# Dealing the last zero fill to the transfer engines in four arcs instead of two pieces

## The chip, the cores and the metric

One core of a Trainium2 chip. A core has five engines with queues of their own (TensorE or PE, VectorE or DVE, ScalarE or ACT, GpSimd or POOL, SyncE or SP) and 16 transfer engines that carry all DMAs, numbered 0 to 15 here. A DMA is issued by one of the queues, cut into packets, and the packets are dealt to the transfer engines. The metric is device microseconds of one execution, from the outside; the profile's span, from the first to the last instruction, is a little shorter. An engine "carries" a row when the packets of this row are in its queue.

## The reference

One decode step of a transformer block with adaptive layer norm, forward and backward: the outputs are the block's result and the gradients of it in all ten inputs, in bfloat16.

```python
mod = silu(c) @ w_mod                        # six rows of 1024
h = layernorm(x) * (1 + ca) + sa
q = h @ wq                                   # 32 heads of 128
k, v = the last 4096 of 65536 positions of k_cache, v_cache (4 heads, each used by 8 of q)
x = x + ga * (softmax(q k^T * 128**-0.5) v) @ wo
h = layernorm(x) * (1 + cb) + sb
x = x + gb * ((sigmoid(h @ w_gate) * (h @ w_up)) @ w_down)
out, vjp = jax.vjp(block, ...);  return (out, *vjp(grad_out))
```

Only the last 4096 positions of the caches are read, so the gradients of the caches (out_2 and out_3 of the kernel, 4 heads x 65536 x 128 each) are zero at the first 61440 positions of each head. These zeros are 126 MB of the 185.6 MB that the kernel writes to memory.

## The kernel before, in words

All of it is one long program for one core, in an order written out by hand (`tc.manual_schedule()`): no planner and no loop over tiles decides when something runs. Weights and caches are loaded into one big on-chip tile (`arena`), the forward and backward products run on TensorE, gradients of the weights are outer products that VectorE and ScalarE write into buffers in `arena`, and DMAs store the buffers. Nearly all of these DMAs are issued from GpSimd's queue, some from SyncE's.

Between them come the zeros. They are cut into 120 regions of 1 MB, kept in the list `zleft`; `zero(n)` (line 186) takes the next n regions and issues their fill on GpSimd's queue. Calls of `zero` are strewn over the whole program with counts from tables (`Z_N`, `Z_B`, `Z_ROWS` and others), so that fills are issued where the queues have room. A fill is a DMA from a region already zero to the next (first from an on-chip tile of zeros, later, when `from_dram[0]` is set, from the first region filled, `zero_src`).

Seven of the 120 regions are "narrow": they are 128 rows of 8 KB, with 120 KB from row to row. Their indices in the list are in `NARROW`. Of a narrow region, rows 8 to 127 are filled by the fill proper; rows 0 to 7 of all seven are filled by `zero_rest` (line 424) and by small head DMAs. A narrow fill is there to give the transfer engines unequal work:

- line 193 resets the cursor that says on which transfer engine the next DMA from GpSimd begins;
- line 196 issues the head, a DMA of 256-byte pieces with an outer size of 5 (`NS`), or of 7 (`NL`) in the last narrow fill. An outer size of n takes n engines in a row, and the cursor goes on by n;
- the first six narrow fills then issue 120 rows with an outer size of 60 (line 209). This goes to 15 engines, 8 rows each, beginning at engine 5, and so leaves out engine 4 (`SKIP`);
- the last one (`n == nlen - 1`, lines 200 to 207) issues two pieces. Each is a view `(t p) x -> p t x` with `t = 3`, so its outer size is the rows divided by 3. The first has 72 rows, outer size 24, and goes to 12 engines from engine 7 on (7 to 15 and 0 to 2), 6 rows each. The second has 48 rows, outer size 16, and goes to all 16, 3 rows each. Engines 3 to 6 (`LIGHT`) therefore carry 3 rows, the other twelve 9.

This last narrow fill is the last entry of `zleft`. It is issued by `zero(Z_ROWS[1])` (line 1339), after the store of a piece of the gradient of w_up (`dw_rows`, line 1142) and ahead of the stores of the gradient of wo (`dwo`, line 1274). After it 56 more DMAs go out, 43 of GpSimd (`dw_rows`, `dwo`, `sec` at line 1269, `dwq_tile` at 1315, `s2` at 1319, `kv_store` at 1311) and, near the end, 13 of SyncE. These have an outer size of 128 and load all 16 engines alike, but for three tiny ones with 8 rows (line 308). The last are stores of the key gradient, two from GpSimd's queue and two from SyncE's.

Of the kernel before, what the change touches and what calls it, by code (L numbers as in the profile page):

```python
# [11 lines left out]
FP32 = mybir.dt.float32  # L12
# [22 lines left out]
SCALE = DH ** -0.5  # L35
KIB = 512
SKIP = 4
LIGHT = (3, 4, 5, 6)
NARROW = (15, 45, 75, 93, 103, 113, 119)

# [21 lines left out]
def kernel(  # L63
# [91 lines left out]
    def as_rows(piece, n):  # L155
        return piece.rearrange("i (p x) -> (i p) x", p=n)
# [9 lines left out]
    nlen = len(NARROW)  # L166
    ncount = list(range(1, nlen + 1))
    NS = SKIP + 1
    NL = LIGHT[-1] + 1
    rest = out_2[0, 0, 0:SKW, :].rearrange("r d -> (r d)").rearrange("(p x) -> p x", p=P)[0:8, 0:nlen * ZW].bitcast(FP32)  # L170
    assert nlen * 2 <= 20

# [2 lines left out]
    zero_rows = zero_src[:, 0:P * ZW // 4].rearrange("i (p x) -> (i p) x", p=P).bitcast(FP8)  # L175

    def pairs(rows):
        return rows.rearrange("(t p) x -> p t x", t=2)

    def dep(later, earlier):  # L180
        tc.add_manual_dep(later.ins, earlier.ins.name,
                          mybir.DependencyInfo(mybir.DependencyClass.Sync, mybir.DependencyReason.DATA),
                          reason="pace")

    def zero(n, after=None, big=False):
        for _ in range(n):
            if len(zleft) <= keep[0]:
                return
            region, narrow_ = zleft.pop(0)  # L190
            first = None
            if narrow_:
                nc.gpsimd.inc_swdge_sem([], [], mode="reset_dge_cursor")
                n = nlen - ncount.pop()
                ns = NL if n == nlen - 1 else NS
                first = nc.gpsimd.dma_start(
                    out=rest[0:ns, 0:nlen * 128].rearrange("p (t x) -> p t x", t=2)[:, :, n * 64:(n + 1) * 64],
                    in_=(zero_rows[0:ns, 0:128].rearrange("p (t x) -> p t x", t=2) if from_dram[0] else
                         zeros[0:ns, 0:64].rearrange("p (t x) -> p t x", t=1).broadcast_to([ns, 2, 64])))
                if n == nlen - 1:  # L200
                    a0 = 8
                    for rows in (6 * (16 - len(LIGHT)), 3 * 16):
                        ins = nc.gpsimd.dma_start(
                            out=region[a0:a0 + rows, :].bitcast(FP32).rearrange("(t p) x -> p t x", t=3),
                            in_=zero_rows[0:rows, :].rearrange("(t p) x -> p t x", t=3))
                        a0 += rows
                    assert a0 == P and from_dram[0]
                else:
                    ins = nc.gpsimd.dma_start(
                        out=pairs(region[8:P, :].bitcast(FP32)),  # L210
                        in_=(pairs(zero_rows[0:120, :]) if from_dram[0] else
                             zeros[0:60, :].rearrange("p (t x) -> p t x", t=1).broadcast_to([60, 2, ZW // 2])))
            elif big and region.shape[0] == 1:
                ins = nc.gpsimd.dma_start(  # L214
                    out=as_rows(region, BIGP).bitcast(FP32),
                    in_=zero_src[:, 0:P * ZW // 4].rearrange("i (p x) -> (i p) x", p=BIGP).bitcast(FP8))
            else:
                if region.shape[0] == 1:
                    region = as_rows(region, P)
                if from_dram[0]:  # L220
                    ins = nc.gpsimd.dma_start(out=pairs(region.bitcast(FP32)), in_=pairs(zero_rows))  # L221
                else:
                    ins = nc.gpsimd.dma_start(out=region.bitcast(FP32), in_=zeros[:, :])
            if after is not None:
                dep(first or ins, after)
# [198 lines left out]
    def zero_rest(after):  # L424
# [3 lines left out]
        dep(ins, after)  # L428
        for n0, n1, ns in ((0, nlen - 1, NS), (nlen - 1, nlen, NL)):
            nc.gpsimd.dma_start(  # L430
# [120 lines left out]
    for j in range(KD):  # L551
        if j in (1, 2, 3):
            kT_unit(8 + 2 * j)
            kT_unit(9 + 2 * j)
        if 0 < j <= NT:
            for g in range(G):
                wqT_unit(j - 1, g, "AVAA"[g])
        for b in range(2):
            mm = rows_mm(q_ps[b], h1_bf[:, j:j + 1], heads(wq_t[j])[:, 16 * b:16 * b + 16, :], j == 0, j == KD - 1)
        zero(Z_Q[j], mm)  # L560
# [14 lines left out]
    for ch in range(8):  # L575
        ps = new_ps("sc_ps")
        for g in range(G):
            mm = nc.tensor.matmul(ps[32 * g:32 * g + 32, 0:512], lhsT=q_col2[:, HG * g:HG * g + 32],
                                  rhs=k_T[:, g, ch * 512:(ch + 1) * 512], start=True, stop=True,
                                  tile_position=(0, 32 * g))  # L580
        nc.scalar.copy(out=P_bf[:, ch * 512:(ch + 1) * 512], in_=ps[:, :])
        nc.vector.reduce_max(out=mx8[:, ch:ch + 1], in_=ps[:, :], axis=AX.X)
        zero(Z_KC[ch], mm)
# [25 lines left out]
    rsum = vt([P, 1], "rsum")  # L609
    last = nc.vector.reciprocal(out=rsum, in_=ssum)  # L610
    zero(Z_SM, last)
    from_dram[0] = True
    rs_ps = new_ps("rs_ps")[:, 0:P]
# [709 lines left out]
    for b in range(2):  # L1323
        do4 = new_ps("do4")
        for i in range(KD):
            for a in range(4):
# [4 lines left out]
                       in_=do4.rearrange("q (a h r) -> q a h r", a=4, h=4))  # L1331
# [189 lines left out]
```

## Time and profile before

| | before |
|---|---|
| time, median of 3 runs | 592.18 us (592.12 to 592.22) |
| the profiled execution's own time | 592.17 us |
| its span | 590.4 us |
| PE, DVE, ACT, POOL busy | 73%, 60%, 42%, 26% |
| moved | 246.04 MB in 32030 packets, mean 417 GB/s |
| memory read, written | 88.50 MB, 185.60 MB |
| last narrow fill issued | 459.2 us (head), 460.0 and 460.8 us (the two pieces) |
| its pieces, issue to landing | 10.7 and 10.8 us |
| last compute | about 569 us |

The page gives DMA's busy share as the mean over the 16 transfer engines, so one engine that is busy while the others are done shows as a sixteenth. The queues q0 and q1 are the DMAs of GpSimd and of SyncE; q8 and q14 load instructions. In the table by stretches each row has the stretch, its length, the busy time of PE, weight loads, DVE, ACT and POOL with the number of instructions, then TensorE's granted clock, DMA's share and GB/s. DMA's share can be a little over 1, where packets of two queues overlap.

### The profile page before, as it was taken

The page shows a single profiled execution, that of the slowest core. Times are in us where ns is not written, and L with a number is a line of the kernel's source. Part 1 is how long each engine was busy: PE and PEld are TensorE (multiplying, and loading weights), DVE is VectorE, ACT ScalarE, POOL GpSimd, SP SyncE. Part 2 cuts the span into 40 slices and gives each one's busy share as a digit, 9 for nine tenths or more (in the row PEclk, how much of TensorE's full clock was granted, in tenths as well). Part 3 has the DMA queues.
Part 4 walks back from the last instruction along what each step waited for, and adds up shares of the span by engine and source line. Part 5 has one row for each costly group of instructions (what it writes and reads, how often), then busy time and mean ns, then how long its engine had stood idle before and what let it go on. Part 6 is the DMA issues. An engine that isn't in the chain of part 4 may idle for free.

```text
span 590.4 us, 10143 instructions
## 1 busy us (share of the span) xinstructions
PE 429.2 (73%) x4160; PEld 244.6 (41%) x4160; DVE 354.2 (60%) x646; ACT 248.3 (42%) x398; POOL 152.2 (26%) x253
## 2 busy tenths in 40 slices
PE   3998689999999999997977756665684437175410
PEld 2884333323334545543544645554572336013100
DVE  3765579988931103019471866888886967655750
ACT  2579510545541103411223655666572446074410
POOL 3113214122122212222222322333312733132100
PEclk9997689999999999999998768878757756655555
DMA  8999999999999999999999999999999999999998
GB/s 350 422 419 421 422 455 427 423 428 431 427 399 465 402 443 440 399 441 435 416 391 405 418 412 408 402 411 397 420 420 425 423 426 424 422 418 415 414 412 340
DMA packets 32030, 246.04 MB, mean 417 GB/s; under 512 B 4898, under 2 KB 4904, under 8 KB 16680
## 3 DMA queue, kind: packets, MB, share of 16 engines
q0 software_dynamic: 26992, 225.98, 95.1%
q1 hardware_dynamic: 4944, 19.41, 9.3%
q8 instruction: 32, 0.52, 0.3%
q14 instruction: 14, 0.11, 0.0%
q10 hardware_dynamic: 48, 0.01, 0.0%
HBM read 88.50 MB, written 185.60 MB: 464 GB/s over the span
## 4 chain that ended last, share of the span: by engine, by line
PE 40%; DMA 26%; DVE 17%; ACT 9%; issue 4%; POOL 1%; ACTq 0%; POOLq 0%; DVEq 0%; SPq 0%
PE b_ps L808 15%; DMA out_dram<-arena 12%; PE n_ps L749 9%; DMA arena<-in_B_w_gate_dram 5%; DVE arena L263 4%; DVE arena L250 4%; PE t_ps L703 4%; DMA arena<-in_w_mod_dram 3%; ACT arena L1306 3%; DVE arena L267 3%; DMA arena<-in_B_w_down_dram 2%; DMA out_dram<-out_dram 2%; ACT arena L541 2%; DVE scr L267 2%; PE tp_k L520 1%
## 5 line engine op out<-in xcount | busy, mean ns | idle before, releaser
L808 PE MATMUL b_ps<-arena 128*128 128x512 bf16 x512 | 117.5, 382 | 1.1 <-ACT arena L952 1.1
L250 DVE TENSOR_TENSOR arena<-arena 128x2048 bf16<-128x2048 bf16 (+1 forms) x67 | 78.2, 1177 | 9.0 <-PE n_ps L749 5.2
L952 ACT COPY arena<-tp_side 128x1024 bf16<-128x1024 bf16 x62 | 61.0, 1016 | 52.2 <-PE tp_side L951 51.4
L808 PEld LDWEIGHTS <-arena 128*128 128x128 bf16 x512 | 48.7, 99 | 57.6 <-issue 4.6
L749 PE MATMUL n_ps<-arena 128*128 128x512 bf16 x256 | 67.6, 389 | 3.0 <-DVE arena L250 2.5
L214 POOL DMA_DIRECT2D out_dram<-out_dram x72 | 35.7, 497 | 128.7 <-PE n_ps L749 60.9
L951 PE MATMUL tp_side<-ident_bf,arena 128*128 128x128 bf16 x496 | 49.9, 267 | 9.5 <-DVE arena L250 5.8
L263 DVE TENSOR_SCALAR arena<-arena,slab 128x3584 bf16<-128x3584 bf16 (+2 forms) x40 | 43.5, 1124 | 21.5 <-DMA out_dram<-arena 21.5
L951 PEld LDWEIGHTS <-arena 128*128 128x128 bf16 x496 | 41.8, 123 | 18.3 <-issue 8.5
L711 ACT CAST arena<-t_ps 128x512 bf16<-128x512 f32 x56 | 29.0, 599 | 39.9 <-PE t_ps L703 39.9
L1302 PE MATMUL ps_kv<-arena 32*128 32x512 bf16 x64 | 26.6, 582 | 25.8 <-DVE arena L271 10.0
L267 DVE CUSTOM_DVE_ANT_0 arena<-arena,scr 128x1024 bf16<-128x1024 bf16 x35 | 40.8, 1224 | 0.2
L1306 ACT ACTIVATE arena<-ps_kv 128x512 bf16<-128x512 f32 x48 | 25.0, 716 | 36.0 <-PE ps_kv L1302 18.7
L749 PEld LDWEIGHTS <-arena 128*128 128x128 bf16 x256 | 21.5, 99 | 35.5 <-issue 19.0
L267 DVE CUSTOM_DVE_ANT_0 scr<-arena,b1k 128x1024 bf16<-128x1024 bf16 x28 | 34.2, 1223 | 3.2 <-DMA arena<-in_B_w_down_dram 2.8
L259 DVE CAST arena<-b_ps 128x512 bf16<-128x512 f32 x6 | 4.2, 692 | 48.8 <-PE b_ps L808 48.8
L221 POOL DMA_DIRECT2D out_dram<-out_dram x31 | 18.9, 612 | 30.1 <-DVE rows_all L250 24.4
L703 PE MATMUL t_ps<-arena 128*32 128x512 bf16 x256 | 24.1, 399 | 2.8 <-ACT arena L772 2.8
L1302 PEld LDWEIGHTS <-arena 32*128 32x128 bf16 x64 | 6.8, 112 | 44.4 <-issue 43.6
L541 ACT COPY arena<-tp_wq 128x1024 bf16<-128x1024 bf16 x23 | 21.5, 1071 | 7.3 <-PE tp_wq L539 7.3
L1089 ACT COPY arena<-tp_ug 128x1024 bf16<-128x1024 bf16 x21 | 20.5, 1009 | 6.7 <-PE tp_ug L1088 6.7
L977 POOL DMA_DIRECT2D arena<-in_B_w_up_dram x14 | 10.8, 773 | 42.3 <-DVE slab L267 21.6
(268 smaller groups left out, 659.3 us busy)
## 6 DMA issues: line engine op xcount, KB each, us to landing
out_dram<-arena POOLq DMA_DIRECT2D x35, 1024.0 KB, 14.1
out_dram<-out_dram POOLq DMA_DIRECT2D x31, 1024.0 KB, 13.1
out_dram<-arena POOLq DMA_DIRECT2D x16, 896.0 KB, 17.3
out_dram<-zeros POOLq DMA_DIRECT2D x10, 1024.0 KB, 10.7
arena<-in_A_wq_dram POOLq DMA_DIRECT2D x8, 1024.0 KB, 20.9
arena<-in_A_wo_dram POOLq DMA_DIRECT2D x8, 1024.0 KB, 12.4
arena<-in_w_mod_dram POOLq DMA_DIRECT2D x7, 1024.0 KB, 18.7
arena<-in_B_w_up_dram POOLq DMA_DIRECT2D x14, 512.0 KB, 10.2
```

What stands on the lines that cost most here:

```text
L214: ins = nc.gpsimd.dma_start(out=as_rows(region, BIGP).bitcast(FP32), in_=zero_src[:, 0:P * ZW // 4].rearrange("i (p x) -> (i p) x", p=BIGP ...
L250: return nc.vector.tensor_tensor(out=out, in0=a, in1=b, op=op)
L263: return nc.vector.tensor_scalar(out=out, in0=a, scalar1=s1, scalar2=None, op0=op0)
L267: return nc.vector.tensor_tensor_reduce(out=out, in0=w, in1=b, scale=1.0, scalar=0.0, op0=ALU.mult, op1=ALU.add, accum_out=acc)
L541: nc.scalar.copy(out=blk, in_=tp[:, :])
L703: nc.tensor.matmul(ps[32 * hh:32 * hh + 32, :].rearrange("p (j m) -> p j m", j=4), lhsT=N_sb[:, h * P + a:(h + 1) * P - 3 + a:4], rhs=a4[: ...
L749: mm = nc.tensor.matmul(nbank[k][:, :], lhsT=k_nat[:, g, t_ * DH:(t_ + 1) * DH], rhs=vp[:, t_ % 2, 4 * k:4 * k + 4, :].rearrange("p h d -> ...
L808: mm = nc.tensor.matmul(bbank[p][k][:, :], lhsT=a4[:, p, h, :], rhs=wo_t[u][:, a, k * 512:(k + 1) * 512], start=(i == 0 and a == 0), stop= ...
L951: nc.tensor.transpose(tp[:, i * P:(i + 1) * P], blk[:, i * P:(i + 1) * P], ident_bf[:, :])
L952: nc.scalar.copy(out=blk if dst is None else dst, in_=tp[:, :])
L1302: nc.tensor.matmul(ps[:, :], lhsT=rows[r, t8 * P:(t8 + 1) * P], rhs=bd[r, :], start=True, stop=True, tile_position=(32 * tc_, 0))
L1306: nc.scalar.activation(out=o, in_=v, func=ACT.Copy, scale=float(scale))
```

## The change

The last narrow fill is issued as four DMAs instead of two. `ARCS` lists, in the order of the cursor, how many engines a piece is for and how many rows each of them gets. The view is the same, with `t` equal to the rows of an engine, so that the outer size of a piece is its number of engines. The head still has an outer size of 7, so the first piece begins at engine 7.

| piece | engines | rows each | rows |
|---|---|---|---|
| (2, 11) | 7, 8 | 11 | 22 |
| (6, 7) | 9 to 14 | 7 | 42 |
| (4, 11) | 15, 0, 1, 2 | 11 | 44 |
| (4, 3) | 3 to 6 | 3 | 12 |

The 120 rows, their source and their place in GpSimd's queue are the same.

```diff
-LIGHT = (3, 4, 5, 6)
+FIRST = 7
+ARCS = ((2, 11), (6, 7), (4, 11), (4, 3))
...
-    NL = LIGHT[-1] + 1
+    NL = FIRST
...
                 if n == nlen - 1:
                     a0 = 8
-                    for rows in (6 * (16 - len(LIGHT)), 3 * 16):
+                    for engines, each in ARCS:
+                        rows = engines * each
                         ins = nc.gpsimd.dma_start(
-                            out=region[a0:a0 + rows, :].bitcast(FP32).rearrange("(t p) x -> p t x", t=3),
-                            in_=zero_rows[0:rows, :].rearrange("(t p) x -> p t x", t=3))
+                            out=region[a0:a0 + rows, :].bitcast(FP32).rearrange("(t p) x -> p t x", t=each),
+                            in_=zero_rows[0:rows, :].rearrange("(t p) x -> p t x", t=each))
                         a0 += rows
```

## The prediction

> **What bounds the kernel now.** I read the page first: the time slices, then the queues. The digits are DMA's busy share of each fortieth of the span, and below them what it moved.
>
> ```profile
> DMA  8999999999999999999999999999999999999998
> GB/s 350 422 419 421 422 455 427 423 428 431 427 399 465 402 443 440 399 441 435 416 391 405 418 412 408 402 411 397 420 420 425 423 426 424 422 418 415 414 412 340
> ...
> q0 software_dynamic: 26992, 225.98, 95.1%
> q1 hardware_dynamic: 4944, 19.41, 9.3%
> q8 instruction: 32, 0.52, 0.3%
> ```
>
> The transfer engines are busy from the first slice to the last; no compute engine is over 73%. So this kernel ends when the last of 16 transfer engines has emptied its queue, and what counts is how evenly the work lies on them. The table by stretches shows how it ends (the last two columns are DMA's share and GB/s):
>
> ```profile
> 475.00:500.00 25.00, 14.72 (x240) 13.65 (x244) 17.74 (x31) 14.45 (x21) 8.15 (x11) 0.57 1.01 424
> ...
> 565.00:570.00 5.00, 0.60 (x2) 0.00 (x0) 3.94 (x7) 0.60 (x1) 0.51 (x1) 0.50 1.01 419
> 570.00:580.00 10.00, 0.00 (x0) 0.00 (x0) 0.00 (x0) 0.00 (x0) 0.54 (x2) 0.50 1.01 411
> 580.00:585.00 5.00, 0.00 (x0) 0.00 (x0) 0.00 (x0) 0.00 (x0) 0.00 (x0) 0.50 1.03 423
> 585.00:588.00 3.00, 0.00 (x0) 0.00 (x0) 0.00 (x0) 0.00 (x0) 0.00 (x0) 0.50 0.84 350
> 588.00:590.40 2.40, 0.00 (x0) 0.00 (x0) 0.00 (x0) 0.00 (x0) 0.00 (x0) 0.50 0.03 14
> ```
>
> Compute is over by 570 us; from there on stores drain at full rate until 585, at 0.84 until 588, and then nearly nothing moves. The trace's packet records give the end more finely. They do not name the engine, but while an engine is loaded its next packet starts 3 or 4 ns before the last one ends, so packets can be linked into 16 chains. From about 473 us to 585 us there are always 16 packets under way. The chains end at 585.20, 585.32, then thirteen of them from 587.51 to 588.34, and one alone at 589.11. That last chain sets the end: 1.28 us later the span of 590.39 closes. One engine is thus 0.77 us behind the second last, and two are 3 us ahead of the rest.
>
> Where the fill is issued, GpSimd's timeline (start, length, count, idle before it) and the fill's own line:
>
> ```profile
> 459.20 0.78 POOL L196 DMA_DIRECT2D out_dram<-out_dram  x1
> 459.98 1.59 POOL L203 DMA_DIRECT2D out_dram<-out_dram  x2
> 461.56 4.35 POOL L1274 DMA_DIRECT2D out_dram<-arena  x3
> 467.23 0.53 POOL L1274 DMA_DIRECT2D out_dram<-arena  x1 [1.32 <-DMA out_dram<-arena]
> 469.35 1.03 POOL L1274 DMA_DIRECT2D out_dram<-arena  x1 [1.59 <-DVE arena L263]
> ```
>
> ```profile
> L203 POOL DMA_DIRECT2D out_dram<-out_dram x2: 783/796/809, 460.0 to 460.8; - x2
> ...
> DMA to landing us min/median/max: 10.7/10.7/10.8
> ```
>
> ```profile
> L1274 POOL DMA_DIRECT2D out_dram<-arena x8: 533/652/3288, 461.6 to 489.0; - x8
> ...
> DMA to landing us min/median/max: 11.6/14.3/18.6
> ```
>
> The reader sees that the two pieces take 0.80 us of GpSimd each, and that this and the stores behind it land 10.7 to 18.6 us after issue: about that much work stands in the queues.
>
> **The change, part by part.** Rows per engine, before: 6 of the 72-row piece on engines 7 to 15 and 0 to 2, and 3 of the 48-row piece on all, so 9, and 3 on engines 3 to 6. After: 11 on six of them (7, 8, 15, 0, 1, 2), 7 on 9 to 14, 3 on 3 to 6. The sum is 120 both times (12x9 + 4x3; 6x11 + 6x7 + 4x3), so no byte is added: two rows move from each of six engines to each of six others.
>
> *A row's price.* 419 GB/s in the stretch 565 to 570 is 26.2 GB/s for each of 16 engines, so a row of 8 KB takes 8192/26.2 = 0.313 us; the links of a chain give 0.306 (packets of 8192 bytes start 306 ns apart). I take 0.31; two rows are 0.62 us. From 473 us on the engines are never without a packet, so these 0.62 us go unchanged through the 115 us that follow to that engine's end.
>
> *The end.* It depends on which group the last chain (589.11) is in.
> - In 3 to 6: it stays at 589.11. The worst that a lifted engine can do is 588.34 + 0.62 = 588.96, still before it. Change 0.
> - In 7, 8, 15, 0 to 2: 589.73, change +0.62.
> - In 9 to 14: it falls to 588.49; the next is a lifted one at up to 588.96, so the change is between -0.15 and -0.62.
>
> Followed back to the fill, the last chain looks like one of the four that carry no row of the 72-row piece, which is engines 3 to 6. Two chains can cross within a nanosecond and be swapped, and some are, so this is a lean and no proof; it is why I take 0. Of the two early chains nothing is gained: they wait for the last whatever they carry.
>
> *Two more issues on GpSimd.* 2 x 0.80 = 1.6 us of its time at 460 us, ahead of the eight stores of L1274, the stores of L1142 that are queued between them, and what follows on its queue; SP's queue holds nothing at that time. Hidden: those stores wait 11.6 us or more in the queues before they land, so being issued 1.6 us later only makes that wait shorter. The trace also shows GpSimd's transfers using eight completion semaphores in turn, so a transfer waits for the eighth before it. The reset's head and its pieces now take five of the eight places for 1 MB instead of three. The third store of L1274 then waits for a store issued at 458.59 instead of 449.84, and may go out some 5 us later than its 465.4 (an estimate: the landing of 11.6 us added to 458.59 gives 470.2). Behind that transfer are then the fill and two stores of 1 MB, about 7 us at 423 GB/s, less up to 4 us by which some chains are ahead of others there. Cover remains, though less. Lower bound 0. If it is gone, the engines stand idle for up to the added 1.6 us: upper bound +1.6. I take 0, since 16 packets are under way throughout and the landing rows are far above the delay. Who waits for these stores is VectorE, which reuses their buffers; it idles 21.5 us for DMA in the last 130 us already and has the order of the queue, not the issue time, to thank for it.
>
> *More completions.* Each transfer ends with 16 packets of 4 bytes; two more transfers add 32, which start about 6 ns apart: 0.01 us if spread, 0.2 us if all fall on one engine. I take 0.01, because the before's own completions are spread over the chains.
>
> *Sum:* 0 + 0 + 0.01 on the profiled execution's 592.17 us (span 590.39 and 1.78 around it), which is 0.01 below the median of 592.18. Forecast 592.2.
>
> [...]
>
> **The rivals.**
> *A late engine is loaded further (slower side, within the bound).* The last chain is 7, 8, 15 or 0 to 2, for instance because an engine that the deal holds for light is slow by itself. Price 0.62: 592.8. For it: six of 16 engines are in that group. Against: the chain looks like one without the six rows.
> *The late engine is relieved.* It is one of 9 to 14: 591.55 to 592.0, middle 591.8. For it: again six of 16. Against: the same.
> *The queue runs dry (slower).* Place: 468 to 473 us, where five of the eight places hold 1 MB. It decides when what stands in the queue of the engines furthest ahead falls under the delay of the stores. Price up to 1.6: 593.8. For it: GpSimd already waits for DMA there (1.32 us before the fourth store), and one store takes 3.288 us to issue. Against: 7 us of work less 4 us of lead.
> *The deal isn't what it says.* The four pieces would have to start each where the one before ended. If all began at engine 7, engines 7 and 8 would carry 11 + 7 + 11 + 3 = 32 rows instead of 9: 23 x 0.31 = 7.1 us late, less the 0.77 of a chain that isn't the last: 598.5. Against: before, the 72-row piece starts behind the seven engines of the small head in the records, four chains without it; the cursor is thus kept between transfers.
> *The odd packets fall elsewhere.* 32 instruction loads of 16 KB take about 1 us each of one engine, and the last chain has one of them at 487.3 us. With other code they may fall on other engines: the end then moves between 588.34 and 589.9 by itself, 591.4 to 593.0.
>
> **How the numbers follow.** Unchanged end (592.2): 0.46. Loaded further (592.8): 0.21. Relieved (591.8): 0.13. Odd packets (591.4 to 593.0): 0.08. Queue dry (593.8): 0.07. Wrong deal (598.5): 0.02. What is left, 0.03, I give to a faster end by more than I can find a reason for. 0.2% is 1.18 us, about what a measurement of this kernel tells from no change: 591.0 to 593.36. The first four cases lie inside: 0.88. Slower 0.09, faster 0.03. Range 591.5 to 593.1: it holds the unchanged, loaded and relieved cases and most of the odd packets, and leaves out the dry queue and the wrong deal.
>
> **What would show it.** Right: L203 (under its new line) four times, GpSimd 0.8 us each; 16 packets under way all through; the drain after 570 us the same, the last chain within 0.7 us of 589.1. Wrong: a DMA share under 1.00 in the stretch 460 to 500; or one engine's packets going on for several us after the others have ended; or the early chains gone and the late ones with them.

## The result: 1.7 us slower, outside the predicted range

| | before | after |
|---|---|---|
| median, 16 runs each, taken together | 591.96 us (591.55 to 592.28) | 593.64 us (592.93 to 596.96) |
| ratio | | 1.0039, 95% interval 1.0026 to 1.0051 |
| profiled execution | 592.17 us, span 590.4 | 593.8 us, span 591.7 |
| time outside the span | 1.78 us | 2.12 us (median) |
| last of 16 chains of packets ends | 589.11 us | 590.28 us |

Thirteen of the 16 times of the changed kernel lie between 592.93 and 594.88 us, three between 596.71 and 596.96. The profiled execution is one of the many.

The page of the changed kernel, slices and queues:

```profile
DMA  8999999999999999999999999999999999999997
GB/s 347 421 418 420 421 451 426 431 431 430 426 395 463 407 445 425 405 438 434 431 382 410 417 412 407 395 410 405 421 421 425 420 426 417 417 417 412 413 413 328
DMA packets 32430, 246.04 MB, mean 416 GB/s; under 512 B 5298, under 2 KB 5304, under 8 KB 17080
...
q0 software_dynamic: 27392, 225.99, 95.0%
```

The bytes are the same and the transfer engines are still the bound. But there are 400 more packets (32030 before), all on GpSimd's queue and all under 512 B. I had counted 32. The rest is filling: a piece that goes to n < 16 engines puts on each of the others as many packets of 4 bytes as one of its own engines gets rows. Before, that was 6 x 4 = 24 for the first piece and none for the second; now 11 x 14 + 7 x 10 + 11 x 12 + 3 x 12 = 392. The difference of 368 and the 32 completions make 400. Two other deals below have the counts that this gives, 32398 and 32062 packets (same_rows_four and two_more_even). So has the kernel before: of its 4182 packets of 4 bytes on GpSimd's queue 245 x 16 = 3920 are completions, and 262 are the filling of its seven heads (6 x 22 + 18), of the six narrow fills with 8 rows on each of 15 engines (48), of the first piece (24) and of two small DMAs of `zero_rest` (26 + 14). What the counts show is on how many engines a piece goes and how many rows each gets. The engines' numbers are those of the kernel's own count from the reset, and no record names an engine. That each piece begins where the one before ended is not in the counts either; but had all begun at engine 7, two engines would have ended some 7 us late by my estimate, and the 16 chains end within 3.5 us.

The fill's line and GpSimd's timeline in the changed kernel (first: durations min/median/max; then start, length, count, idle before):

```profile
L205 POOL DMA_DIRECT2D out_dram<-out_dram x4: 767/805/905, 460.6 to 463.1; - x4
```

```profile
460.58 3.27 POOL L205 DMA_DIRECT2D out_dram<-out_dram  x4
465.38 0.71 POOL L1276 DMA_DIRECT2D out_dram<-arena  x1 [1.53 <-DVE arena L265]
467.82 0.56 POOL L1276 DMA_DIRECT2D out_dram<-arena  x1 [1.73 <-DMA out_dram<-arena]
469.93 2.65 POOL L1276 DMA_DIRECT2D out_dram<-arena  x3 [1.54 <-DVE arena L265]
```

Four issues of 0.8 us, as forecast. The stores of dwo (L1274 before, now L1276) go out later: the first three at 461.56, 464.84 and 465.38 before, at 465.38, 467.82 and 469.93 now. The third is 4.5 us late.

The end of the changed kernel, by stretches:

```profile
475.00:500.00 25.00, 14.72 (x236) 13.63 (x237) 17.71 (x31) 14.27 (x21) 8.44 (x11) 0.56 1.01 422
...
580.00:585.00 5.00, 0.00 (x0) 0.00 (x0) 0.00 (x0) 0.00 (x0) 0.00 (x0) 0.50 1.03 421
585.00:588.00 3.00, 0.00 (x0) 0.00 (x0) 0.00 (x0) 0.00 (x0) 0.00 (x0) 0.50 0.90 377
588.00:591.70 3.70, 0.00 (x0) 0.00 (x0) 0.00 (x0) 0.00 (x0) 0.00 (x0) 0.50 0.22 89
```

No engine runs dry for a time that counts (the share stays at 1.01 and above until 585; by the packet records 16 packets are under way at every moment from 460 to 473 us, and fewer in 0.2% of the time from 473 to 585, 0.1% in the kernel before), and yet more is left at the end: 0.22 of 3.7 us after 588, where before it was 0.03 of 2.4. (The share goes over 1 on one queue too: from 475 to 500 us GpSimd's packets alone make 1.009 in the kernel before, and within a chain a packet starts 3 or 4 ns before the last one ends, on one queue as on two.) The packets linked into chains say more. The 16 chains now end in two groups of eight, at 586.76 to 588.44 and at 589.40 to 590.28; their mean is 588.62 instead of 587.73. So 0.9 us of the 1.17 us by which the last end moved is work that all engines do later, and 0.27 is a wider spread.

Where the 0.9 us arose, I read from the packet records: the bytes not yet moved at a given time, as time at 419 GB/s, after minus before. It is 0.12 at 5 us already (other kernels' profiled executions have up to 0.1 us there, and up to 0.5 us at 460 us, ahead of the fill, so only what is added from then on counts), 0.15 at 464, 0.31 at 472, 0.36 at 496, 0.68 at 512 and 0.87 at 560 to 584. So a sixth of a microsecond comes with the fill and a third between 496 and 512, where nothing of the change runs any more. In that stretch packets of 8 KB took 319 ns on the mean instead of 311, as this row of after and this of before show (417 against 424 GB/s at the same share):

```profile
500.00:510.00 10.00, 3.27 (x38) 1.36 (x38) 6.15 (x8) 3.02 (x7) 2.78 (x5) 0.85 1.02 417
```

```profile
500.00:510.00 10.00, 3.20 (x37) 1.26 (x37) 5.94 (x8) 2.84 (x6) 3.54 (x5) 0.84 1.01 424
```

### The profile page after: what moved, and what is told of

Read it like the earlier page. It is cut to its first block, busy times and chain, and to the rows that moved or that the text cites. A ratio compares the mean times of both kernels' runs of the same rounds, so it can differ in the third digit from the quotient of the medians.

```text
span 591.7 us, 10145 instructions
## 1 busy us (share of the span) xinstructions
PE 429.4 (73%) x4160; PEld 243.2 (41%) x4160; DVE 354.1 (60%) x646; ACT 247.8 (42%) x398; POOL 150.7 (25%) x255
## 2 busy tenths in 40 slices
DMA packets 32430, 246.04 MB, mean 416 GB/s; under 512 B 5298, under 2 KB 5304, under 8 KB 17080
## 4 chain that ended last, share of the span: by engine, by line
PE 42%; DMA 23%; DVE 16%; ACT 9%; issue 5%; POOL 1%; ACTq 0%; POOLq 0%; DVEq 0%
PE b_ps L810 15%; DMA out_dram<-arena 14%; PE n_ps L751 9%; DMA arena<-in_B_w_gate_dram 5%; DVE arena L252 4%; PE t_ps L705 4%; DVE scr L269 3%; DMA arena<-in_w_mod_dram 3%; DVE arena L265 3%; ACT arena L1308 3%; ACT arena L543 2%; DVE arena L269 2%; PE tp_side L953 2%; PE fg L1067 1%; PE tp_k L522 1%
## 5 line engine op out<-in xcount | busy, mean ns | idle before, releaser
L1304 PE MATMUL ps_kv<-arena 32*128 32x512 bf16 x64 | 26.6, 581 | 26.4 <-DVE arena L265 10.2
```

Source lines behind the costliest of these rows:

```text
L1304: nc.tensor.matmul(ps[:, :], lhsT=rows[r, t8 * P:(t8 + 1) * P], rhs=bd[r, :], start=True, stop=True, tile_position=(32 * tc_, 0))
```

## The experiments

Times are medians; each is compared with runs of the kernel before taken beside it (592.02 to 592.23 us). "Outside" is time less span.

| kernel | pieces of the last fill | time, us | ratio, 95% interval | outside, us |
|---|---|---|---|---|
| same_rows_four | 4 | 598.73 | 1.0069 to 1.0133 | 2.12 |
| two_more_even | 4 | 597.12 | 1.0073 to 1.0099 | 2.15 |
| new_rows_base | 4 | 594.73 | 1.0039 to 1.0064 | 2.12 |
| mirrored | 4 | 600.24 | 1.0076 to 1.0141 | 2.12 |
| same_rows_broken | 4 | 593.32 | 1.0009 to 1.0027 | 2.08 |
| change_broken | 4 | 593.40 | 1.0014 to 1.0032 | 2.12 |
| two_more_broken | 4 | 593.19 | 1.0012 to 1.0030 | 2.11 |
| mirrored_broken | 4 | 593.09 | 1.0009 to 1.0028 | 2.10 |
| before_broken | 2 | 591.80 | 0.9986 to 1.0003 | 1.80 |
| two_arcs | 2 | 591.92 | 0.9989 to 1.0006 | 1.78 |
| before_moved | 2, later | 591.58 | 0.9986 to 1.0004 | 1.80 |
| change_moved | 4, later | 592.75 | 1.0006 to 1.0024 | 2.13 |
| three_broken | 3 | 591.99 | 0.9990 to 1.0008 | 1.99 |
| six_broken | 6 | 597.66 | 1.0082 to 1.0110 | 1.76 |
| split_earlier | 2, and 2 more transfers elsewhere | 592.29 | 0.9995 to 1.0012 | 2.11 |
| merged | 2, and 2 fewer elsewhere | 591.85 | 0.9989 to 1.0007 | 1.78 |
| six_parted | 6, in pairs | 592.47 | 0.9995 to 1.0013 | 1.77 |
| change_parted | 4, in pairs | 592.67 | 0.9999 to 1.0016 | 2.11 |

### The rows, the pieces or the issues?

Four kernels that change only the table of arcs:

```diff
-ARCS = ((2, 11), (6, 7), (4, 11), (4, 3))
+ARCS = ((2, 9), (6, 9), (4, 9), (4, 3))          # same_rows_four
+ARCS = ((12, 6), (16, 1), (16, 1), (16, 1))      # two_more_even
+ARCS = ((2, 8), (6, 4), (4, 8), (16, 3))         # new_rows_base
+ARCS = ((2, 7), (6, 11), (4, 7), (4, 3))         # mirrored
```

> Four arcs as in the change, but with the rows per engine of before: 9 on 7 to 15 and 0 to 2, 3 on 3 to 6 (pieces 2x9, 6x9, 4x9, 4x3). Rows theory (the new dealing is the cause): no different from before within 0.3 us. Pieces theory (a piece for n engines puts as many 4-byte packets on each of the other 16-n engines as rows on its own; that filling is the cause): 360 such packets against 392 in the change and 24 before, so +1.3 to +1.6 us; the page should count 32398 packets (32030 + 336 + 32 for two more transfers). Issue theory (two more transfers on GpSimd's queue are the cause): +1.5 us.

> The 72-row piece of before (12 engines, 6 rows each), then the 48 rows as three transfers of 16 rows, one row for each engine, instead of one of 48. Rows per engine as before, two more transfers as in the change, hardly any filling (24 packets, page 32062). Rows theory: as before within 0.3 us. Pieces theory: as before within 0.3 us. Issue theory: +1.5 us, and the stores of L1276 go out 2 to 5 us later than before, as in the change.

> The rows per engine of the change (11 on six, 7 on 9 to 14, 3 on 3 to 6) with less filling: pieces 2x8, 6x4, 4x8 and then 3 rows on all 16. Filling 248 packets, page 32286. Rows theory: slower than before by as much as the change, 1.3 to 1.7 us. Pieces theory: +0.9 to +1.1 us. Issue theory: +1.5 us.

> The change turned round: 7 rows on 7, 8, 15, 0 to 2, 11 rows on 9 to 14, 3 on 3 to 6, in the same four arcs. Filling 328 packets, page 32366. Rows theory in its simple form (too much on 7, 8, 15, 0 to 2): as before or up to 0.5 us faster; if any move away from the even dealing hurts: +0.5 to +1.5 us. Pieces theory: +1.2 to +1.4 us. Issue theory: +1.5 us.

New rows aren't needed for a loss: with the very rows of the kernel before, same_rows_four loses 6.7 us. Nor is the filling needed: two_more_even has none beyond the 24 packets of before, and loses 5.1. new_rows_base, with the change's rows and 248 filling packets, loses 2.7. What is left is the two issues, at up to four times the most I had allowed for them. GpSimd's timeline of same_rows_four, and then VectorE's:

```profile
459.49 0.78 POOL L197 DMA_DIRECT2D out_dram<-out_dram  x1
460.26 11.83 POOL L205 DMA_DIRECT2D out_dram<-out_dram  x4
472.09 2.73 POOL L1276 DMA_DIRECT2D out_dram<-arena  x5
```

```profile
461.67 0.18 DVE L261 CAST slab<-do_ps 128x32 bf16<-128x32 f32 x1
461.77 3.25 DVE L265 TENSOR_SCALAR arena<-scr,slab 128x1024 bf16<-128x1024 bf16 x8
464.93 0.18 DVE L261 CAST arena<-dq_ps 128x32 bf16<-128x32 f32 x1
465.03 1.67 DVE L265 TENSOR_SCALAR arena<-scr,slab 128x1024 bf16<-128x1024 bf16 x4
466.62 1.15 DVE L265 TENSOR_SCALAR arena<-arena,slab 128x3584 bf16<-128x3584 bf16 x1
467.68 1.67 DVE L265 TENSOR_SCALAR arena<-scr,slab 128x1024 bf16<-128x1024 bf16 x4
469.26 1.15 DVE L265 TENSOR_SCALAR arena<-arena,slab 128x3584 bf16<-128x3584 bf16 x1
470.32 1.67 DVE L265 TENSOR_SCALAR arena<-scr,slab 128x1024 bf16<-128x1024 bf16 x4
```

The four issues take 11.83 us instead of 3.2. By single records the third begins at 461.87, just as the cast on VectorE ends, and ends at 465.14, just as the next cast ends; the fourth begins there and ends at 472.10, 0.1 us after the last of 14 outer products in a row (471.99). An issue of GpSimd can thus be *held* while VectorE runs one outer product after another, and comes free when the row breaks. The 3.288 us store of the kernel before, which I had quoted without asking what it waited for, is the same thing: begun at 461.56, as a cast ended, and free at 464.85, with the next:

```profile
461.38 0.19 DVE L259 CAST slab<-do_ps 128x32 bf16<-128x32 f32 x1
...
464.64 0.19 DVE L259 CAST arena<-dq_ps 128x32 bf16<-128x32 f32 x1
```

In same_rows_four the queues meanwhile run dry, as the stretch shows, the second row being that of before:

```profile
460.00:475.00 15.00, 4.87 (x73) 4.22 (x70) 11.99 (x29) 5.78 (x7) 15.00 (x11) 0.69 0.78 297
```

```profile
460.00:475.00 15.00, 4.98 (x72) 4.27 (x69) 12.73 (x29) 5.70 (x7) 9.99 (x11) 0.69 1.06 423
```

A share of 0.78 and 297 GB/s, against 1.06 and 423 before. Of 15 us that is a good 4 us lost at once.

A hold here spans 8 to 14 products, and an issue that takes 0.8 us free takes 3.3 to 7.0 us in it (3.27 and 6.96 in same_rows_four). By what the products hold it no run shows.

Most issues in such a row are not held that long. The first two pieces of same_rows_four, beside products too, take 0.82 and 0.79 us, and in the profiled execution of the changed kernel a piece that begins at 462.18, just after the same cast as in same_rows_four, takes 0.905 us. But in the single records of seven profiles (before, after, the four kernels of this round and two_arcs below) all 49 issues between 459 and 473 us that run beside these products and take over 0.6 us end 0.10 to 0.13 us after the end of one of them, while the stores with no product beside them take 0.53 to 0.61. So an issue that takes that long here comes free only behind a product, most of them soon, a held one not before many have passed. What decides which is held no run shows.

Where an execution was profiled, its time fits the holds in it: 594.10 in new_rows_base with one of 3.29 us, 597.23 in two_more_even with one of 4.63 us late in the row, 600.47 in same_rows_four and 600.29 in mirrored with two, of 3.3 and 7.0 us. The other times of these kernels (594.43 to 594.84, 597.1 to 597.3, 600.2 to 600.91) lie near these three, and may have the same reasons; they were not profiled.

### Taking the hold away

Between the outer products of dwo a sum of two numbers on VectorE, whose result nobody uses:

```diff
         for a in range(4):
             outer_dve(wo_t[u][:, a, :], o_perm[:, 8 * a + u:8 * a + u + 1], dattn_b)
+            nc.vector.reduce_sum(out=crumb, in_=rm, axis=AX.X)
```

> The four pieces with the rows of the kernel before (9, 9, 9 and 3), and after each outer product of dwo a sum over two numbers on VectorE (24 to 32 of them, some 0.1 us each), so that no unbroken run of its bfloat16 products lasts longer than about 1.6 us. Held-issue theory: an issue of GpSimd that begins inside such a run waits until the run breaks, so the 3.27 and 6.96 us issues at 461.9 and 465.1 us become 2 us at most, the stretch 460 to 475 is back at a DMA share over 1.03, and the time falls from 598.7 to between 592.0 and 594.8, without the second group of times near 600. Theory of the transfers themselves (two more transfers, 368 more packets of 4 bytes): nothing changes, 597 to 600.5. If the products of VectorE have nothing to do with it and GpSimd is held by the transfers in flight (a full ring of descriptors), also no change.

> The change itself (11, 7, 11, 3) with the same sums between the products. Held-issue theory: its times near 597 are executions in which an issue was held long, and they go; the rest of its loss (593.6 against 592.0) stays, because in its profiled execution no issue near the fill was held: 592.5 to 593.8. Theory that the loss is held issues altogether: 592.0 within 0.3. If the sums cost something by themselves, before_broken shows it.

> The kernel before with the same sums between the products: the control. Its one held issue (3.288 us at 461.6) should become 1.7 us or less; what it delayed was covered by 10 us of work in the queues, so the time should stay at 592.0 within 0.4. If it falls under 591.5 the held issue had cost something before the change too; if it rises over 592.5 the sums cost something.

same_rows_broken takes 593.32 us instead of 598.73, and its eleven times lie between 592.86 and 594.18, all below the lowest of same_rows_four (594.43). Its stretch of the fill:

```profile
460.00:475.00 15.00, 5.07 (x73) 4.33 (x70) 14.48 (x57) 5.76 (x7) 8.84 (x13) 0.57 1.06 419
```

The share is back at 1.06, and no issue between 459 and 475 us takes over 1.5 us. So the row of products is what holds the issues, and the held issues are what cost same_rows_four the 5 us. before_broken stays where before was: the held store of before had cost nothing, and its queues were not dry meanwhile (1.06 in its row above). In change_broken the ten times lie between 593.12 and 593.80, without one near 597. This is what the theory wants, but with three such times in 16 it could be chance as well (13/16 to the tenth power is 0.13), and none of the three was profiled. And it settles that the hold isn't what the changed kernel usually loses: 593.40 is still 1.3 us over before.

### What the remaining 1.2 us are not

> The kernel before's rows (9 and 3) in two pieces that lie side by side, ((12, 9), (4, 3)): as many transfers and issues as before, and 12 x 3 + 4 x 9 = 72 filling packets instead of 24, so 32078 packets. Every theory that blames the number of issues: 592.0 within 0.4. A theory that blames pieces lying side by side (each engine's rows in one lump, instead of six and three with the other piece between) gives 593 or more.

> The kernel before's rows in four pieces that nest ((12, 6), (16, 1), (16, 1), (16, 1)), so two more transfers but only the 24 filling packets of before, with the sums between the products of dwo. Without the sums it took 597.12. Held-issue theory: the 4.63 us issue at 467.6 goes and the time falls under 594. What it is then tells apart the 1.2 us that same_rows_broken still lost: if the 368 filling packets cost that, this kernel is back at 592.0 within 0.4; if two more transfers cost it (they take two of the eight completion semaphores, and the stores behind go out later), it is at 593.3 within 0.4.

> The opposite deal (7, 11, 7, 3) with the sums. Rows theory: if the engines given 11 rows decide the end, this deal and the change's (593.40 with the sums) differ by a good part of 0.62 to 1.24 us, and one of them is under same_rows_broken (593.32). Theory that the rows hardly matter and the four pieces do it: 593.3 within 0.4, as the other two.

```diff
+ARCS = ((12, 9), (4, 3))                         # two_arcs, without the sums
+ARCS = ((12, 6), (16, 1), (16, 1), (16, 1))      # two_more_broken
+ARCS = ((2, 7), (6, 11), (4, 7), (4, 3))         # mirrored_broken
```

Two pieces side by side cost nothing (591.92), although in this kernel, too, a store is held, for 4.66 us at 467.35. Three stores had gone out ahead of it; in two_more_even, held for 4.63 us at 467.63, it was one. Four pieces without filling are at 593.19, so the filling isn't the 1.2 us. The opposite deal is at 593.09, with the change's at 593.40 and the even one at 593.32: if the engines with 11 rows set the end, the two opposite deals would stand up to 1.24 us apart. They stand 0.3 apart, which these intervals don't tell from nothing. The deal of rows, which my prediction was mostly about, hardly matters; no run shows which engine is the late one.

### Elsewhere, fewer, more

The last narrow fill issued some 12 us later, ahead of dwo(3):

```diff
-Z_ROWS = (1, 1, 0, 0, 0, 0, 0, 0)
+Z_ROWS = (1, 0, 1, 0, 0, 0, 0, 0)
```

> The change, with the last narrow fill issued some 12 us later (ahead of dwo(3) instead of ahead of dwo(2), dwo(0), dwo(4)), where VectorE's products come singly and the queues are full to the limit of the eight semaphores. Place theory (two more issues cost because of where they stand): 592.0 to 592.7, and no execution near 597. Theory that two more transfers cost 1.2 us wherever they stand, or that the deal of rows does: 593.2 to 593.8.

> The control for change_moved: the two pieces of the kernel before at that later place. All theories: 592.0 within 0.5, unless the place itself costs; change_moved is then to be held against this time.

At that place both medians are lower (before_moved's interval holds 1), but four pieces still cost 1.17 us more than two. My theory of the place fell. In all runs with two more transfers, however, 0.3 us of the loss lies outside the span (2.08 to 2.15 us instead of 1.75 to 1.80). So I asked for the price of a transfer, with three and six pieces, with two ordinary fills issued as halves, and with two pairs of ordinary fills as one transfer each (all with the sums):

```diff
+ARCS = ((12, 6), (16, 1), (16, 2))                                   # three_broken
+ARCS = ((12, 3), (4, 1), (12, 3), (4, 1), (12, 3), (4, 1))           # six_broken
 # split_earlier: the 13th and the 21st fill of this kind
-                    ins = nc.gpsimd.dma_start(out=pairs(region.bitcast(FP32)), in_=pairs(zero_rows))
+                    fills[0] += 1
+                    for a0, a1 in (((0, 64), (64, 128)) if fills[0] in SPLIT else ((0, 128),)):
+                        ins = nc.gpsimd.dma_start(out=pairs(region[a0:a1, :].bitcast(FP32)), in_=pairs(zero_rows[a0:a1, :]))
 # merged: two neighbouring regions, twice
...
+                ins = nc.gpsimd.dma_start(
+                    out=as_rows(whole2[i0:i0 + 2, :], P).bitcast(FP32).rearrange("(t p) x -> p t x", t=2),
+                    in_=zero_rows.rearrange("p (o x) -> p o x", o=1).broadcast_to([P, 2, ZW // 2]))
...
```

> Three pieces ((12, 6), (16, 1), (16, 2)), one more transfer than before, with the sums between the products. Two more cost 1.1 to 1.3 us wherever they stood, 0.33 of it outside the span. If each transfer has its price, this kernel takes half: 592.4 to 592.8, with 1.95 us outside the span. If a limit of the number of transfers is crossed (a ring or a table that is full), it is 592.0 or 593.2 and the time outside the span 1.78 or 2.12, with nothing between.

> Six pieces (12 and 4 engines in turn, 3 and 1 rows each time), four more transfers than before, the same rows, 72 filling packets. A price for each transfer: 594.2 to 594.8 and 2.45 us outside the span. A limit that is crossed once: 593.2 within 0.4 and 2.12 outside.

> The last fill as before, but two ordinary fills between 340 and 450 us issued as two halves each, 64 rows and 16 engines, so no filling packets and no uneven work: two more transfers at another place. A price for each transfer: 593.2 within 0.4, and 2.12 us outside the span. If only transfers of the last fill cost (uneven arcs, the stores behind it late), 592.0 within 0.4; the time outside the span tells that part by itself.

> The last fill as before, but two pairs of neighbouring 1 MB fills after 400 us issued as one transfer of 2 MB each, so two transfers fewer than before. A price for each transfer: 590.6 to 591.2 and 1.45 us outside the span, which would beat both kernels. A limit that is crossed: 592.0 within 0.4. Against it stands only that a transfer of 2 MB fills a place of the eight twice as long.

There is no price per transfer; both theories of this round missed. Inside the span, two more transfers elsewhere cost nothing (split_earlier: median span 590.2 against 590.3 us), three pieces nothing, four 0.7 to 1.0 us, six 5.6. Outside it, one more transfer gives 1.99 us, two 2.1, four 1.76 again, two fewer 1.78. The 0.33 us outside the span thus goes with the number of transfers, wherever they are, but not in proportion; what happens there no record shows.

Six pieces have no held issue in 459 to 475 us. GpSimd's timeline, and the stretch 468 to 472 us of six_broken and of before:

```profile
458.79 0.68 POOL L1144 DMA_DIRECT2D out_dram<-arena  x1 [3.48 <-DVE arena L265]
459.45 0.91 POOL L197 DMA_DIRECT2D out_dram<-out_dram  x1
460.36 2.85 POOL L205 DMA_DIRECT2D out_dram<-out_dram  x4
464.62 0.88 POOL L205 DMA_DIRECT2D out_dram<-out_dram  x1 [1.42 <-DMA out_dram<-out_dram]
467.25 0.63 POOL L205 DMA_DIRECT2D out_dram<-out_dram  x1 [1.75 <-DMA out_dram<-arena]
469.52 3.44 POOL L1278 DMA_DIRECT2D out_dram<-arena  x5 [1.64 <-DVE slab L1277]
```

```profile
468.00:472.00 4.00, 0.00 (x0) 0.00 (x0) 4.00 (x11) 0.79 (x2) 2.48 (x4) 0.67 0.67 244
```

```profile
468.00:472.00 4.00, 0.00 (x0) 0.00 (x0) 3.84 (x9) 0.00 (x0) 2.57 (x3) 0.65 1.04 421
```

This is the eight semaphores at work: in the kernels before and after, each transfer of GpSimd that has an eighth before it (237 and 239) is issued 0.28 us or more after that one has landed. The fifth and the sixth piece wait for transfers to land, and the first store goes out at 469.52, 8 us later than before. The eighth transfer ahead of it is the store issued at 458.79; the trace has it land 10.2 us after its issue, at 469.0, and the first store follows 0.6 us later, as the third store of the changed kernel (469.93) follows the landing of the store issued at 459.20 (10.2 us, 469.4). Behind it stands nothing but the fill, less than 1 MB in all. So the queues are dry: a share of 0.67, and the work left, against before, grows by 2.0 us from 464 to 472. (The timeline names one of the sums as releaser. But the store's own products were done long before, since before_broken, with the same sums, issues this store at 461.70; the landing fits.) Nor does the loss end there: with the stores flowing again, packets of 8 KB took 338 ns in 472 to 476 us and 327 in 476 to 480, against 309 before, and by 584 another 2.5 us had been lost.

### The same pieces, not in a row

Two pieces where the fill was, two behind the store of dwo(0), and in six_parted two more behind that of dwo(5):

```diff
                     for engines, each in ARCS:
...
+                        pieces.append(piece)
+                    ins = two_pieces()
...
     dwo(0)
     do_bf = vt([P, HQ], "do_bf", BF16)
     cp(do_bf, do_ps)
+    two_pieces()
     dwo(4)
...
+    two_pieces()
     dwo(6)
```

> The six pieces of six_broken (597.66), issued two at a time: two where the fill was, two behind the store of dwo(0), two behind that of dwo(5), so that 1 MB stores stand between them in the eight places. Theory of the eight places (a transfer waits for the eighth before it, and small pieces in a row leave little work in the queues): the DMA share of 460 to 475 is back over 1.04 and the time falls by most of 5.6 us, to 592 to 593.5. Theory that six uneven pieces cost by themselves (skew between the engines, filling): 596.5 to 598.

> The change's four pieces, two where the fill was and two behind the store of dwo(0), with the sums. change_broken took 593.40, of which 0.33 lies outside the span and 0.9 to 1.0 in it. Theory of the eight places: the part in the span goes, the part outside stays: 592.2 to 592.7, span 590.1 to 590.6. Theory that the four uneven pieces or the rows cost it: 593.2 to 593.7. If the cursor did not stay between the pairs, the second pair's rows would lie on wrong engines, up to 8 rows or 2.5 us too much on one: over 594.5 and one group of engines ending late.

```profile
468.00:472.00 4.00, 0.55 (x5) 0.28 (x3) 4.00 (x13) 1.50 (x2) 2.69 (x4) 0.50 1.03 423
```

This is six_parted in the same stretch: 1.03 and 423 GB/s. It takes 592.47 us instead of 597.66, with the same six pieces, rows and filling. change_parted takes 592.67 instead of 593.40: its span's median is 590.6 against 590.4 of before, 0.2 us longer where change_broken's was 1.0 longer, and the 0.33 outside the span stay. So what six pieces cost inside the span comes from their standing in a row in the eight places, not from being many or uneven, and of what four cost most goes with it too. The profiled executions agree: from 460 us to 584 the work left, against before, grows by 0.7 us in the changed kernel, 0.5 in change_broken and 0.1 in change_parted. But a rival is left for the four. Two of the pieces also go out 3 to 4 us later, and by the medians of before_moved and before a later place alone may be worth 0.4 us; the fill of before in parted pieces was not run.

For six pieces the trace also shows how. What GpSimd had issued and the engines had not yet moved (the sizes of the issues less the packets) falls in six_broken to 0.07 MB, in six_parted only to 1.4. For four this figure shows no such difference: it falls to 1.5 MB in change_broken and to 1.7 in change_parted. Nor is it the third store's lateness, since in change_parted it goes out at 469.73, as late as in the changed kernel. In change_moved the four stand in a row again, only later, which would be why it lost there too; that wasn't tried apart.

What makes the packets of 8 KB slower 30 us on, in kernels whose engines don't run dry, stays open. In 500 to 510 us they take 319 ns in the changed kernel, 322 in same_rows_broken, 317 in mirrored_broken, and 314 in change_broken and two_more_broken, against 310 in change_parted and 311 in before. So four pieces in a row at this place go with slower packets, but by very unequal amounts. That the chains end in two groups of eight is no sign of it: they do so in six_parted (310 ns) and don't in mirrored_broken. The trace names neither the engines nor the reason.

No version beat both kernels: two_arcs, before_broken, before_moved and merged are 0.2 to 0.4 us under before, and all four intervals hold 1.

## Why the prediction was wrong, by its own steps

- *The bound* was read rightly: the transfer engines, with no slack at the end. A share over 1.00 all through, however, did not mean no loss. At 1.02 and 1.01 it held 417 and 424 GB/s.
- *The deal* is what the diff says (32430 packets come out of its count), and *the end* as a question of which group is last was the wrong question: with the sums, equal, changed and mirrored rows end within 0.3 us. Which engine was last in before, on which I leaned for my 0, no run shows.
- *More completions* was mis-sized: 400 small packets, not 32. At 464 to 472 us they go with some 0.16 us of lost work, near the upper end I gave to them (0.2). In two_more_broken, which has no filling, that figure is 0.05, and in same_rows_broken, which has 336 more of it, 0.12: a tenth of a microsecond or so is theirs. At the 6 ns that I took for one, 400 shared by 16 engines make 0.15.
- *Two more issues on GpSimd* is the step that failed. I had each part in hand: 1.6 us of issues (measured: 1.68 more), the eight semaphores, five of eight places for 1 MB, the third store at an estimated 470.2 us (measured 469.93), GpSimd's wait for DMA there, and the 3.288 us store. Then I wrote "I take 0", because 16 packets under way seemed to be all that counts. The 16 packets stayed under way, as forecast, and four pieces in a row still cost 0.7 to 1.0 us inside the span, whatever their rows and filling (with the sums; 1.3 in the changed kernel's profile). The step from "no engine idles" to "no cost" is what failed. Why the packets then take longer is open.
- Its *upper bound of 1.6* was no bound either. It took the delay for the length of two issues. A held issue takes up to 7.0 us, and the eight places held the stores back by up to 8 us, so relatives of this change lose 5 to 8 us.
- *Outside the span* I carried the 1.78 us over as a constant. It became 2.12, a fifth of the loss. That goes with the two more transfers, since split_earlier has it too; the reason is open.
- *The queue runs dry*, with a chance of 0.07, has the right price (593.8) by luck. I had made it of engines idle for the length of two issues, and in the profiled execution no queue runs dry; its 1.63 us are made otherwise, as said below. Place and mechanism were those of relatives: with six pieces or a held issue the queues do run dry in the stretch I named, 468 to 473 us.
- *What would show it* could not see this loss. Four issues of 0.8 us and 16 packets under way came as signs of being right, and no share under 1.00 as a sign of being wrong. Only the end told: the last chain came 1.17 us later instead of within 0.7, and the drain was not the same.

The sum of the profiled executions, 593.8 less 592.17, is 1.63 us. It is made of 0.33 outside the span and 1.3 in it, of which the mean end of the engines is 0.9, their spread 0.27 and the closing behind the last packet the rest.

## What to carry to other kernels

Where a kernel is bound by its transfers, don't ask only how many bytes each engine gets, but how much work the limited number of transfers in flight (eight of GpSimd's here) holds at the change's place: six small transfers in a row used up places until the queue behind them was dry (5.6 us), and the same ones with large transfers between them cost almost nothing (0.3 us inside the span). Nor is it enough that every engine has work: four in a row cost up to 1.0 us with all of them busy. Look at any GpSimd issue that takes several times its median (3.288 against 0.652 us for the stores of dwo before), see what VectorE does meanwhile, and ask what would happen if the next issue were caught. Compare the time outside the span as well.

## What was unexpected of the hardware

- A DMA issue on GpSimd beside a row of bfloat16 outer products on VectorE is now and then held until the row breaks: 3.3 us for 8 products, 7.0 for 14. The holds of 3.3 us ended with a cast from PSUM (0.18 us) between two rows; with a sum over two numbers (0.15 us) behind each product no issue near the fill took over 1.5 us. All 49 issues over 0.6 us beside such products, held or not, ended 0.10 to 0.13 us after the end of one of them.
- A GpSimd transfer on n of 16 engines brings packets of 4 bytes for all the others, one for each row of one of its own engines: 392 here, by the packet counts (32430 in all, against 32030 before).
- At the same DMA share, 1.01 to 1.02 in 500 to 510 us, an 8 KB packet took 309 to 322 ns, 314 and more only where four or more pieces had stood in a row at 460 us; right behind a dry stretch (share 0.99) it was 338.
- The time outside the span goes with the number of transfers, and not in order: 1.78, 1.99, 2.1 and 1.76 us with none, one, two and four more.
